# Eight groups of keys transposed by DMA, a later first output projection, and x normalised in place

## The chip, the cores and the metric

The kernel runs on one core of a Trainium2 chip. The metric is the device time of one execution in microseconds. Engines are named as the profile names them: PE is TensorE (PEld its weight loads), DVE VectorE, ACT ScalarE, POOL GpSimd, SP SyncE. SP, POOL and ACT each issue DMA transfers in their own order: a transfer that must wait holds up everything behind it on the same engine.

## The reference

```python
def reference(A_x, A_k_cache, A_v_cache, A_wq, A_wo, B_x, B_w1, B_w2, B_w3, B_w4):
    x  = A_x                                # [1, 2048, 576] bf16
    xn = _layernorm(x)
    s  = attention(xn, ...) @ wo            # 32 heads of 128, 16 key/value heads, last W = 512 keys, no mask
    # B: a mixer and an MLP on the same xn
    h  = gelu(_layernorm(xn) @ w1)          # 576 -> 576
    # the four column quarters of h are shifted along the sequence by +1, -1, +2, -2 rows
    hs = shifted(h) @ w2
    x1 = xn + hs
    h2 = gelu(_layernorm(x1) @ w3) @ w4     # 576 -> 4608 -> 576
    g  = silu(x1 + h2)
    return x + s * g
```

Each key/value head ("group" below) serves two query heads.

## The kernel before

**Blocks and slots.** The 2048 rows are four query blocks of 512. Attention runs through 4 x 32 = 128 slots, one for each block and head. A slot holds four score matmuls (`stage_s`, L541, 128x512 each), the query projection of the next head (`stage_q`, L507 and L522), sixteen products of probabilities and values (`stage_v`, L560), and, on ACT, four exponentials. The output o of a head is transposed by a DMA on SP into a tile of `oT_pool` (`stage_t`, L573).

**What fills the slots.** The program is written out by hand: `at(u, fn)` puts a step into slot u and `pe(u, atoms)` puts matmuls there, which are dealt out between the slot's own. The steps are the loads of weights, keys, values and x, layernorms, transposes, and the output projection of the block before (`wo_groups`, matmuls at L269): five lists of 32 or 128 matmuls, `main` for each of four row tiles and `rem` for the last 64 columns. For block 0 they stand in slots 34 to 38, for blocks 1 and 2 from the second slot of the block after on. wo itself comes in eight loads on POOL (`load_wo`), each behind `late`: a tiny POOL copy that reads a probability tile of the slot, so that the transfer isn't issued before that slot is reached. The slots for these are 2, 8, 16, 20, 23, 27, 29 and 31. What is queued behind such a copy on POOL waits as well.

**Keys.** Groups 0 to 3 are transposed at the launch. Groups 4 to 15 lie in a stage buffer and are transposed by PE, four transposes a group (`prep_k`, L372) and one DVE copy from PSUM (L376), in slot 2g - 3. Group g is first used in slot 2g.

**Buffers.** `stage_pool` has three buffers of 512 x 640 values. They hold, in turn, the loaded keys, the loaded x of a block, the output projection's result (`so_t`) and, for blocks 2 and 3, the transposed normalised rows for the mixer (`xnnT`, `tr2` at L261); blocks 0 and 1 have `xnnT_pool`. x is loaded into the stage buffer and normalised into `xn_b`. The tail columns 512 to 576 are stored twice in `xn_b` and `xm_b`, after the whole row.

**Mixer.** After slot 127: `b1_pair` and `b1_rest` (first layer; the last 16 columns of each quarter go through `hq` by a DMA transpose on SP, L827), `shifts` (L834, four DVE copies from hq into `hs`, and a DMA on SP that doubles hs, L835), `b2_pair` and `b2_rest` (second layer). Their order is a list with `aside` steps between. w2 (`w2_m`) is loaded by POOL behind a gate copy that waits for the last oT. At the end of the mixer come the last three lists of the output projection of block 3 (L269), and then a gate on POOL (L926) that waits for the last `hs`.

**MLP.** The pools of attention and mixer are closed, and in their memory lie nine sets of weights (`w3_s`, `w3r_s`, `w4_s`, which the profile writes w_s and w3r_s), loaded in order on POOL (L948 w3, L952 the last 64 rows of w3 in two loads, L955 w4). PE runs `up` (L996) and `down` (L1033). SP reloads s and x for the end (L965, L967).

Of the kernel before, what the change touches and what calls it, by code (L numbers as in the profile page):

```python
# [8 lines left out]
P = 128  # L9
# [22 lines left out]
def kernel(  # L32
# [14 lines left out]
    nc = tc.nc  # L47
# [68 lines left out]
    def layernorm_steps(pool, dsts, srcs, twice=False):  # L116
        n = len(srcs)
        hw = D // 2
        st_ = {}

        def stats(i):
            if i == 0:
                st_["mv"] = pool.tile([P, n, 2], FP32, name="ln_mv")
            st = pool.tile([P, 2, 6], FP32, name="ln_st")
            for j in range(2):
                tc.keep_in_program_order(
                    nc.vector.bn_stats(out=st[:, j, :], in_=srcs[i][:, j * hw:(j + 1) * hw]))
            nc.vector.bn_aggr(out=st_["mv"][:, i, :], in_=st[:])

        def inv():  # L130
            st_["r"] = rsqrt_newton(pool, st_["mv"][:, :, 1], n)

        def apply(i):
            parts = [(dsts[i], srcs[i])]
            if twice:
                parts = [(dsts[i][:, 0:D], srcs[i]), (dsts[i][:, D:DP], srcs[i][:, NF * P:D])]
            for dst, src in parts:
                nc.vector.tensor_scalar(out=dst, in0=src, scalar1=st_["mv"][:, i, 0:1],
                                        scalar2=st_["r"][:, i:i + 1], op0=ALU.subtract, op1=ALU.mult)

        return ([lambda i=i: stats(i) for i in range(n)] + [inv] + [lambda i=i: apply(i) for i in range(n)])
# [82 lines left out]

    octx = ctx.enter_context(ExitStack())
    wo_sb = octx.enter_context(tc.tile_pool(name="a_wo", bufs=1, side="right")).tile([P, Hq, D], BF16, name="wo_sb")
    oT_pool = octx.enter_context(tc.tile_pool(name="oT_pool", bufs=36, side="right"))
    fence_pool = ctx.enter_context(tc.tile_pool(name="fence", bufs=2))
    tctx = ctx.enter_context(ExitStack())
    xnnT_pool = tctx.enter_context(tc.tile_pool(name="xnnT_pool", bufs=2))  # L230
    stage_pool = tctx.enter_context(tc.tile_pool(name="stage_pool", bufs=3))
    so_t, oT_t, xnnT = {}, {}, {}
    w1_all = xT_b[0][:].rearrange("p k q -> p (k q)")
    w1_m = w1_all[:, 0:NF * D].rearrange("p (k m) -> p k m", k=NF)
    w1_p = w1_all[:, NF * D:NF * D + 2 * P].rearrange("p (j m) -> p j m", j=2)
    w1_tail = B_w1[NF * P:D, :]
    gate = keep.tile([1, 1], BF16, name="gate")

# [12 lines left out]
    def stage():  # L251
        return stage_pool.tile([P, DP * TB], BF16, name="stage")

    def stage_rows():
        return stage()[:, 0:TB * D].rearrange("p (t d) -> p t d", t=TB)

    def tr2(b, tt):
        if tt == 0:
            xnnT[b] = (xnnT_pool.tile([P, DP * TB], BF16, name="xnnT") if b < 2 else stage())[:].rearrange(
                "p (k t) -> p k t", k=NDC)  # L260
        nc.sync.dma_start(out=xnnT[b][:, :, tt * P:(tt + 1) * P], in_=xm_b[b % 2][:, tt, :], transpose=True)  # L261

    FLAG_OPS = (ALU.max, ALU.min)
# [1 line left out]
    def wo_groups(qb, bank, eng):  # L265
        st = {}

        def mm(ps, h, tt, lo, hi):
            nc.tensor.matmul(ps, lhsT=oT_t[qb * Hq + h][:, tt, :], rhs=wo_sb[:, h, lo:hi], start=(h == 0),  # L269
                             stop=(h == Hq - 1))  # L270

        def main(tt, h):
            if tt == 0 and h == 0:
                so_t[qb] = stage_rows()
            if h == 0:
                st[tt] = bank([P, M0], "pswo")
            mm(st[tt][:, :], h, tt, 0, M0)
            if h == Hq - 1:
                nc.scalar.activation(out=so_t[qb][:, tt, 0:M0], in_=st[tt][:, :], func=ACT.Copy, scale=0.5)
                if qb == NB - 1 and tt == TB - 1:  # L280
                    store()

        def store():
            eng.dma_start(out=rows(s_dram, qb * TB, TB), in_=so_t.pop(qb)[:, :, :])

        def rem(tt, h):
            if tt == 0 and h == 0:
                st["pr"] = bank([P, TB, R0], "pswr")
            mm(st["pr"][:, tt, :], h, tt, M0, D)
            if tt == TB - 1 and h == Hq - 1:  # L290
                nc.scalar.activation(out=so_t[qb][:, :, M0:D], in_=st["pr"][:, :, :], func=ACT.Copy, scale=0.5)
                if qb < NB - 1:
                    store()

        return [[lambda tt=tt, h=h: main(tt, h) for h in range(Hq)] for tt in range(TB)] + [
            [lambda tt=tt, h=h: rem(tt, h) for tt in range(TB) for h in range(Hq)]]


    with ExitStack() as actx:
# [5 lines left out]
        kT = res.tile([P, Hkv, W], BF16, name="kT")  # L305
        v_sb = res.tile([P, Hkv, KCH, VW], BF16, name="v_sb")
        NWQ = 2
        PLAIN = 4
        wq_b = [res.tile([P, NDC, 4 * Dh], BF16, name=f"wq_b{i}") for i in range(NWQ)]
        ri_b = res.tile([P, Hq, TB], FP32, name="ri_b")  # L310
# [13 lines left out]
        x_t = {}  # L324

        def load_x(b, eng):
            xb = stage_rows()
            x_t[b] = []
            for tt in range(TB):
                xt = xb[:, tt, :]  # L330
                t = b * TB + tt
                eng.dma_start(out=xt, in_=x2[t * P:(t + 1) * P, :])
                x_t[b].append(xt)
# [31 lines left out]
        def prep_k(g):  # L365
# [11 lines left out]

            return [lambda kc=kc: tr(kc) for kc in range(KCH)]

        x_t[0] = []  # L380
        x_first = stage_rows()
        hw = D // 2
        nc.scalar.dma_start(out=x_first[:, 0, hw:D], in_=x2[0:P, hw:D])
        nc.sync.dma_start(out=x_first[:, 0, 0:hw], in_=x2[0:P, 0:hw])
# [240 lines left out]

        for b in range(1, NB):
            for i, group in enumerate(wo_atoms(b - 1)):
                pe(b * Hq + (2 if b == 1 else 1) + i, group)
        for b in range(NB):
            cell = []  # L630

            def ln2_step(i, b=b, cell=cell):
                if not cell:
                    cell.append(ln2_stats_steps(b))
                cell[0][i]()

            for i in range(TB + 1):
                at(ln2_at[b] + i // 2, lambda i=i, f=ln2_step: f(i))
            if b + 1 < NB:
                at(x_at[b], lambda b=b: late(pT_t[x_at[b]][0][0:1, 0:1], lambda: load_x(b + 1, nc.gpsimd)))  # L640
                u1 = ln1_at[b]
                later(u1, lambda b=b: ln1_steps(b + 1), 3, apart=4 if b == 1 else 0)
                for tt in range(TB):
                    at(u1 + (3 + tt, 5, 3 + tt // 2)[b], lambda b=b, tt=tt: tr1(b + 1, tt))
            for tt in range(TB):
                at(tr2_at[b] - 2 + tt // 2, lambda b=b, tt=tt: ln2_apply(b, tt))
                at(tr2_at[b] + tt, lambda b=b, tt=tt: tr2(b, tt))
        wo_last = wo_atoms(NB - 1)[0:2]
        wo_last = wo_last[0][0:Hq - 1] + wo_last[1][0:8] + [wo_last[0][Hq - 1], flag_rows] + wo_last[1][8:]
        pe(U - 1, wo_last[0:10])  # L650
# [1 line left out]
        pe(U + 1, wo_last[22:])  # L652
        at(1, rest_twice)
        at(3 * Hq + 12, load_w1)
        pe_late = []
        at(4, lambda: load_k(2))
        at(12, lambda: load_k(3))
        for g in range(Hkv):
            if g % 2 == 0 and g >= 4:
                at(max(2 * g - 8, 3), lambda g=g: load_v(g // 2))  # L660
            if g > 3:
                pe_late.append((2 * g - 3, g))
        for j in range(2, NB * 8):
            at(4 * (j - 1) - 1, lambda j=j: load_wq(j))
        for i, u in enumerate((2, 8, 16, 20, 23, 27, 29, 31)):
            at(u, lambda i=i, u=u: late(pT_t[u][0][0:1, 0:1], lambda: load_wo(i)))
        for b in range(NB):
            at((b + 1) * Hq + 1, lambda b=b: row_range(b))
# [59 lines left out]
    with ExitStack() as bctx:  # L728
# [18 lines left out]
        mctx = ExitStack()  # L747
        mres = pool("m_res", 1, at=mctx)
        w1_q = mres.tile([P, 4, rsz], BF16, name="w1_q")
        w2_m = mres.tile([P, 4, D], BF16, name="w2_m")  # L750
        w2_q = mres.tile([P, D], BF16, name="w2_q")
        hb = mres.tile([P, 4, HW], BF16, name="hb")
        hq = mres.tile([P, HW], BF16, name="hq")
# [112 lines left out]
            nc.vector.tensor_tensor(out=x1, in0=pr[1], in1=gs[:], op=ALU.add)  # L866

        with tc.manual_schedule(engines={SP, POOL, PE, DVE, ACTE}):
            e = small.tile([P, 1], FP32, name="nr_e")
            nc.scalar.activation(out=e[:], in_=so_t[NB - 1][:, 1, 0:1], func=ACT.Gelu_apprx_tanh)  # L870
            for half in range(2):
                nc.gpsimd.dma_start(out=w1_q[HALVES[half], :, :],
                                    in_=w1_tail.rearrange("p (g s) -> p g s", g=4)[:, :, P:c4])
            nc.gpsimd.tensor_copy(out=gate[:, :], in_=oT_t[NB * Hq - 1][0:1, 0, 0:1])
            by_g = B_w2.rearrange("(g s) d -> g s d", s=c4)
            nc.gpsimd.dma_start(out=w2_m[:], in_=by_g[:, 0:P, :].rearrange("g s d -> s g d"))
            for half in range(2):
                for g in range(4):
                    p0 = half * DR + g * rsz
                    nc.gpsimd.dma_start(out=w2_q[p0:p0 + rsz, :], in_=by_g[g, P:c4, :])  # L880
            for t in (hb[:, :, OFF - PAD:OFF], hb[:, :, OFF + S:OFF + S + PAD], hq[:, OFF - PAD:OFF],
                      hq[:, OFF + S:OFF + S + PAD], *[t[:, :, R0:] for t in h4]):
                nc.gpsimd.memset(t, 0.0)
# [3 lines left out]
                   (b2_pair, 3)]  # L887
            ops = [(f, b, p) for f, b in ops for p in range(2)]
            aside = {0: [lambda: b1_rest(0)], 1: [lambda: b1_rest(1)], 2: [lambda: b1_rest(2)],
                     3: [lambda: b1_rest(3), lambda: shifts(0)], 6: [lambda: shifts(1)], 8: [lambda: shifts(2)],  # L890
                     10: [lambda: shifts(3)]}
            pend = None
            for k in range(len(ops) + 1):
# [467 lines left out]
```

## Time and profile before

| | |
|---|---|
| runs shown, us | 827.32, 820.60, 831.24; median 827.32 |
| profiled execution, us | 820.89 |
| its span, us | 819.4 |
| mean granted clock of TensorE | 0.999 |
| PE busy | 806.8 us, 98% |
| DVE, ACT, POOL busy | 449.8, 444.7, 125.5 us |
| bytes by DMA | 79.94 MB, mean 98 GB/s |

The span is the time from the first to the last instruction of the profiled execution; the rest of its time lies outside it. Busy times of engines overlap and are not added up: what counts is which engine is waited for in each stage. In rows of instructions the columns are: start and duration in us, engine, line and operation, output and inputs, count, and in brackets the idle time before and what ended it. A row "DMA to landing" gives the time from issue to the last byte: shortest, median and longest of the DMAs asked for.

### The profile page before, as it was taken

What the parts mean: (1) busy time and instruction counts of PE and PEld (TensorE: products, weight loads), DVE (VectorE), ACT (ScalarE), POOL (GpSimd) and SP (SyncE); (2) the same over time, 40 slices, a digit from 0 to 9 for tenths busy, and PEclk for the clock granted to TensorE, in tenths of its full rate; (3) what the DMA queues carried; (4) which work ended last, traced back from release to release, by engine and by line L of the source; (5) the groups of instructions that cost most, each with busy time, mean ns of one, the idle gap of its engine ahead of it and who ended that gap; (6) DMA issues with size and microseconds to landing.
All of it is one profiled execution on the core that took longest, in us unless ns stands there. A gap on an engine that the chain in (4) does not pass through costs nothing. (4 is left out here: it accounts for less than half of the span.)

```text
span 819.4 us, 19998 instructions
## 1 busy us (share of the span) xinstructions
PE 806.8 (98%) x8205; PEld 528.2 (64%) x8287; DVE 449.8 (55%) x1387; ACT 444.7 (54%) x798; POOL 125.5 (15%) x212
## 2 busy tenths in 40 slices
PE   8999999999999999999999999999999999999997
PEld 5666654656654666645666546555568888888855
DVE  6878644468832579621566526643246636655413
ACT  7888852688833788833888642032233323334520
POOL 3343301111101111100210031155000000000000
PEclk9999999999999999999999999999999999999999
DMA  7999952374721538810674232299100310230101
GB/s 198 164 210 209 200 105 58 91 136 104 136 55 42 113 83 151 159 49 14 132 128 85 47 67 65 61 354 213 53 2 17 87 49 16 48 88 16 44 15 38
DMA packets 131502, 79.94 MB, mean 98 GB/s; under 512 B 107824, under 2 KB 121680, under 8 KB 131408
## 3 DMA queue, kind: packets, MB, share of 16 engines
q1 hardware_dynamic: 117328, 38.54, 26.1%
q0 software_dynamic: 12832, 38.85, 18.8%
q8 instruction: 65, 1.06, 0.6%
q10 hardware_dynamic: 1248, 1.25, 0.5%
q14 instruction: 29, 0.24, 0.2%
HBM read 46.89 MB, written 6.93 MB: 66 GB/s over the span
## 5 line engine op out<-in xcount | busy, mean ns | idle before, releaser
L545 ACT ACTIVATE pT<-sc 128x512 bf16<-128x512 f32 x512 | 287.2, 598 | 98.0 <-PE sc L541 81.6
L560 PEld LDWEIGHTS <-pT 128*128 128x128 bf16 x2048 | 134.5, 98 | 52.8 <-issue 11.5
L541 PE MATMUL sc<-qT,kT 128*128 128x512 bf16 x495 | 165.1, 379 | 0.1
L560 PE MATMUL po<-v_sb,pT 128*128 128x129 bf16 x2048 | 158.2, 220 | 1.0
L996 PE MATMUL ph<-xT_b,w_s 64*128 64x512 bf16 x976 | 140.9, 376 | 0.0
L1033 PE MATMUL pm<-w_s,h 64*128 64x512 bf16 x864 | 134.9, 377 | 0.0
L522 PE MATMUL psq<-xT_b,wq_b 128*128 128x512 bf16 x463 | 123.6, 379 | 2.3
L1033 PEld LDWEIGHTS <-h 64*128 64x128 bf16 x1728 | 102.0, 94 | 27.1
L1014 ACT ACTIVATE h<-ph 128x512 bf16<-128x512 f32 x67 | 39.4, 597 | 138.2 <-PE ph L996 130.6
L565 DVE TENSOR_TENSOR o<-po,ri_b 128x256 bf16<-128x256 f32 x256 | 108.0, 422 | 6.8 <-DVE ri_b L564 0.3
L1033 PE MATMUL pr<-w_s,h 64*128 64x64 bf16 x864 | 111.3, 189 | 0.0
L269 PE MATMUL pswo<-wo_sb,oT 128*128 128x512 bf16 x434 | 101.3, 379 | 0.6
L996 PEld LDWEIGHTS <-w_s 64*128 64x128 bf16 x1152 | 85.3, 94 | 22.3 <-issue 0.6
L269 PEld LDWEIGHTS <-oT 128*128 128x128 bf16 x1024 | 64.6, 98 | 54.3
L522 PEld LDWEIGHTS <-wq_b 128*128 128x128 bf16 x506 | 49.4, 98 | 57.4 <-issue 0.8
L532 DVE CAST qT<-psq 128x512 bf16<-128x512 f32 x64 | 44.1, 689 | 76.5 <-PE psq L507 45.7
L530 DVE TENSOR_TENSOR qT<-psq,rq 128x512 bf16<-128x512 f32 x62 | 42.8, 690 | 62.3 <-ACT pT L545 53.0
L1012 DVE COPY hx<-ph 128x512 f32<-128x512 f32 x55 | 38.1, 692 | 54.7 <-PE ph L996 54.7
L339 POOL DMA_DIRECT2D wq_b<-in_A_wq_dram x30 | 23.2, 772 | 280.0 <-PE sc L541 280.0
L564 DVE RECIPROCAL ri_b<-po 128x2 f32<-128x2 f32 x256 | 42.3, 165 | 34.5 <-PE po L560 29.2
L541 PEld LDWEIGHTS <-kT 128*128 128x128 bf16 x512 | 46.3, 98 | 20.8 <-DVE qT L532 0.3
L512 ACT ACTIVATE rq<-sc 128x512 f32<-128x512 f32 x62 | 33.6, 594 | 8.0 <-PE sc L507 8.0
(171 smaller groups left out, 729.7 us busy)
## 6 DMA issues: line engine op xcount, KB each, us to landing
wq_b<-in_A_wq_dram POOLq DMA_DIRECT2D x30, 512.0 KB, 4.8
wo_sb<-in_A_wo_dram POOLq DMA_DIRECT2D x8, 576.0 KB, 5.6
w_s<-in_B_w_dram POOLq DMA_DIRECT2D x9, 512.0 KB, 9.6
w_s<-in_B_w_dram POOLq DMA_DIRECT2D x10, 288.0 KB, 7.0
w_s<-in_B_w_dram POOLq DMA_DIRECT2D x4, 576.0 KB, 9.4
s_b<-s_dram SPq DMA_DIRECT2D x4, 576.0 KB, 5.5
x_b<-in_A_x_dram SPq DMA_DIRECT2D x4, 576.0 KB, 9.0
out_dram<-o SPq DMA_DIRECT2D x15, 144.0 KB, 1.8
```

Source lines behind the costliest of these rows:

```text
L269: nc.tensor.matmul(ps, lhsT=oT_t[qb * Hq + h][:, tt, :], rhs=wo_sb[:, h, lo:hi], start=(h == 0), stop=(h == Hq - 1))
L522: nc.tensor.matmul(psq[:, :], lhsT=w[:, kc, hh * Dh:(hh + 1) * Dh], rhs=xT_b[qb % 2][:, kc, :], start=(kc == 0 and not (two and hh == 1)), ...
L530: behind["qT"] = nc.vector.tensor_tensor(out=qT[:, :], in0=psq[:, :], in1=rq_t.pop(u)[:, :], op=ALU.add)
L532: nc.vector.tensor_copy(out=qT[:, :], in_=psq[:, :])
L541: nc.tensor.matmul(sc[:, :], lhsT=kT[:, g, kc * P:(kc + 1) * P], rhs=qT_t[u][:, :], start=True, stop=True)
L545: behind["exp"] = nc.scalar.activation(out=pT[:, :], in_=sc[:, :], func=ACT.Exp, scale=SCALE)
L560: nc.tensor.matmul(po[:, j, :], lhsT=pTs[kc][:, tt * P:(tt + 1) * P], rhs=v_sb[:, g, kc, 0:Dh + 1], start=(kc == 0), stop=(kc == KCH - 1))
L564: nc.vector.reciprocal(out=ri, in_=po[:, :, Dh])
L565: nc.vector.tensor_tensor(out=o[:, t0:t0 + 2, :], in0=po[:, :, 0:Dh], in1=ri.unsqueeze(2).to_broadcast([P, 2, Dh]), op=ALU.mult)
L996: nc.tensor.matmul(ps[i][:, :], lhsT=lhsT, rhs=xT[half, kc, :], start=first, stop=last, skip_group_check=True)
L1014: nc.scalar.activation(out=h3[:, :], in_=src[:, :], func=ACT.Gelu_apprx_tanh)
L1033: nc.tensor.matmul(out, lhsT=h3_t[b, fc][half, tt * P:(tt + 1) * P], rhs=w4_s[fc // WS][half, fc % WS, lo:hi], start=key not in started, s ...
```

## The change

Four edits:

1. Keys of groups 8 to 15 are transposed by DMA on SP (`tr_k`) instead of PE and DVE, groups 8 to 11 in slots 8 to 11, and groups 12 to 15 in slots 16 to 19. Groups 4 to 7 remain on PE.
2. The output projection of block 0 moves from slots 34 to 38 to slots 43 to 47, its eight weight loads from slots 2 to 31 to slots 14 to 39, and `oT_pool` grows from 36 to 46 buffers.
3. x is loaded into `xn_b` and normalised there; so the tail columns are written ahead of the whole row. `stage_pool` has two buffers, the output projection's result a pool of its own with one (`so_pool`), and `xnnT` of blocks 0 and 1 comes from `stage_pool`. The transposes into `xnnT` of blocks 2 and 3 move from slots 86 to 95 to the start of the mixer, into tiles of its own. `w2_m` lies in `xT_b[1]` and is loaded in slot 127; the gate before it is gone.
4. The shifted copies of block 0 (`shifts(0)`) stand ahead of `b1_rest(3)`.

```diff
             if twice:
-                parts = [(dsts[i][:, 0:D], srcs[i]), (dsts[i][:, D:DP], srcs[i][:, NF * P:D])]
+                parts = [(dsts[i][:, D:DP], srcs[i][:, NF * P:D]), (dsts[i][:, 0:D], srcs[i])]
...
-    oT_pool = octx.enter_context(tc.tile_pool(name="oT_pool", bufs=36, side="right"))
+    oT_pool = octx.enter_context(tc.tile_pool(name="oT_pool", bufs=46, side="right"))
...
-    xnnT_pool = tctx.enter_context(tc.tile_pool(name="xnnT_pool", bufs=2))
-    stage_pool = tctx.enter_context(tc.tile_pool(name="stage_pool", bufs=3))
+    stage_pool = tctx.enter_context(tc.tile_pool(name="stage_pool", bufs=2))
+    so_pool = tctx.enter_context(tc.tile_pool(name="so_pool", bufs=1))
...
+    w2_m = xT_b[1][:].rearrange("p k q -> p (k q)")[:, 0:4 * D].rearrange("p (k m) -> p k m", k=4)
...
-    def tr2(b, tt):
+    def tr2(b, tt, home=None):
         if tt == 0:
-            xnnT[b] = (xnnT_pool.tile([P, DP * TB], BF16, name="xnnT") if b < 2 else stage())[:].rearrange(
-                "p (k t) -> p k t", k=NDC)
+            xnnT[b] = (home or stage())[:].rearrange("p (k t) -> p k t", k=NDC)
...
-                so_t[qb] = stage_rows()
+                so_t[qb] = so_pool.tile([P, TB, D], BF16, name="so")
...
+        KDMA = 8
...
-            xb = stage_rows()
...
-                xt = xb[:, tt, :]
+                xt = xn_b[b][:, tt, 0:D]
...
+        def tr_k(g):
+            nc.sync.dma_start(out=kT[:, g, :].rearrange("d (kc p) -> d kc p", kc=KCH),
+                              in_=kst_t[g // 4][:, (g % 4) * W:(g % 4 + 1) * W], transpose=True)
+
...
-        x_first = stage_rows()
+        x_first = xn_b[0][:, :, 0:D]
...
-                pe(b * Hq + (2 if b == 1 else 1) + i, group)
+                pe(b * Hq + (11 if b == 1 else 1) + i, group)
...
-                at(tr2_at[b] + tt, lambda b=b, tt=tt: tr2(b, tt))
+                if b < 2:
+                    at(tr2_at[b] + tt, lambda b=b, tt=tt: tr2(b, tt))
...
+        at(U - 1, lambda: nc.gpsimd.dma_start(out=w2_m, in_=w2_by_g[:, 0:P, :].rearrange("g s d -> s g d")))
...
-            if g > 3:
+            if 3 < g < KDMA:
                 pe_late.append((2 * g - 3, g))
+            if g >= KDMA:
+                at(g if g < 12 else g + 4, lambda g=g: tr_k(g))
...
-        for i, u in enumerate((2, 8, 16, 20, 23, 27, 29, 31)):
+        for i, u in enumerate((14, 22, 27, 30, 33, 35, 37, 39)):
             at(u, lambda i=i, u=u: late(pT_t[u][0][0:1, 0:1], lambda: load_wo(i)))
...
-        w2_m = mres.tile([P, 4, D], BF16, name="w2_m")
...
+            for b in range(2, NB):
+                home = mres.tile([P, DP * TB], BF16, name=f"xnnT{b}")
+                for tt in range(TB):
+                    tr2(b, tt, home)
...
-            nc.gpsimd.tensor_copy(out=gate[:, :], in_=oT_t[NB * Hq - 1][0:1, 0, 0:1])
-            by_g = B_w2.rearrange("(g s) d -> g s d", s=c4)
-            nc.gpsimd.dma_start(out=w2_m[:], in_=by_g[:, 0:P, :].rearrange("g s d -> s g d"))
...
-                     3: [lambda: b1_rest(3), lambda: shifts(0)], 6: [lambda: shifts(1)], 8: [lambda: shifts(2)],
+                     3: [lambda: shifts(0), lambda: b1_rest(3)], 6: [lambda: shifts(1)], 8: [lambda: shifts(2)],
```

More of the change, by code (lines that the diff above doesn't have):

```diff
@@ L235 @@
     w1_p = w1_all[:, NF * D:NF * D + 2 * P].rearrange("p (j m) -> p j m", j=2)
+    w2_m = xT_b[1][:].rearrange("p k q -> p (k q)")[:, 0:4 * D].rearrange("p (k m) -> p k m", k=4)
+    w2_by_g = B_w2.rearrange("(g s) d -> g s d", s=c4)
     w1_tail = B_w1[NF * P:D, :]
@@ L252, in stage @@
         return stage_pool.tile([P, DP * TB], BF16, name="stage")
-    def stage_rows():
-        return stage()[:, 0:TB * D].rearrange("p (t d) -> p t d", t=TB)
-    def tr2(b, tt):
+    def tr2(b, tt, home=None):
         if tt == 0:
-            xnnT[b] = (xnnT_pool.tile([P, DP * TB], BF16, name="xnnT") if b < 2 else stage())[:].rearrange(
-                "p (k t) -> p k t", k=NDC)
+            xnnT[b] = (home or stage())[:].rearrange("p (k t) -> p k t", k=NDC)
         nc.sync.dma_start(out=xnnT[b][:, :, tt * P:(tt + 1) * P], in_=xm_b[b % 2][:, tt, :], transpose=True)
@@ L879 @@
                     p0 = half * DR + g * rsz
-                    nc.gpsimd.dma_start(out=w2_q[p0:p0 + rsz, :], in_=by_g[g, P:c4, :])
+                    nc.gpsimd.dma_start(out=w2_q[p0:p0 + rsz, :], in_=w2_by_g[g, P:c4, :])
             for t in (hb[:, :, OFF - PAD:OFF], hb[:, :, OFF + S:OFF + S + PAD], hq[:, OFF - PAD:OFF],
```

## The prediction

> **What bounds the kernel now.** I read the page of the profile first: busy times, then the slices with the granted clock.
>
> ```profile
> span 819.4 us, 19998 instructions
> PE 806.8 (98%) x8205; PEld 528.2 (64%) x8287; DVE 449.8 (55%) x1387; ACT 444.7 (54%) x798; POOL 125.5 (15%) x212
> PEclk9999999999999999999999999999999999999999
> ```
>
> TensorE (PE) is busy for 806.8 of 819.4 us at an undisturbed clock, so only two things can move the end: PE instructions that come or go, and waits in front of PE. The second view is the table of stretches: launch, four attention slots of block 0 with key transposes (67.87 to 79.49), four of block 1 without (155.85 to 167.02), the end of the mixer, and the start of the MLP. After the length come the busy times of PE, PEld, DVE, ACT and POOL, then clock, DMA share and GB/s.
>
> ```profile
> 3.30:12.00 8.70, 7.70 (x89) 5.87 (x88) 7.24 (x21) 5.83 (x13) 0.14 (x1) 1.00 1.03 278
> 67.87:79.49 11.62, 11.52 (x108) 7.23 (x109) 11.41 (x48) 9.97 (x19) 3.83 (x7) 1.00 0.95 163
> 155.85:167.02 11.17, 11.06 (x101) 6.78 (x101) 7.32 (x21) 9.88 (x20) 1.98 (x3) 1.00 0.60 139
> 20.00:70.00 50.00, 49.53 (x458) 31.17 (x467) 39.94 (x130) 43.03 (x78) 22.32 (x37) 1.00 1.17 196
> 526.00:532.00 6.00, 5.95 (x28) 2.71 (x28) 0.00 (x0) 0.33 (x1) 2.73 (x4) 1.00 0.68 136
> 532.00:540.00 8.00, 8.00 (x75) 3.51 (x75) 1.69 (x5) 2.80 (x5) 4.67 (x7) 1.00 1.04 350
> ```
>
> PE fills every stretch except the launch. The other engines have room everywhere but for DVE in block 0 (11.41 of 11.62 us). The DMA engines are full (share 1.0 or more) at the launch, in block 0, and at the start of the MLP, so those are the places where a moved transfer can hurt.
>
> **The change part by part.** *Keys of groups 8 to 15.* Eight groups lose four transposes each: 32 matmuls, 32 weight loads and 8 DVE copies. The matmul's own duration is not the price, because it overlaps its neighbours:
>
> ```profile
> L372 PE MATMUL ps_k<-ident,stage 128*128 128x128 bf16 x48 | 8.6, 219 | 0.0
> 60.68 0.22 PE L372 MATMUL ps_k<-ident,stage 128*128 128x128 bf16 x1
> 60.74 0.38 PE L541 MATMUL sc<-qT,kT 128*128 128x512 bf16 x1
> 61.68 0.27 PE L372 MATMUL ps_k<-ident,stage 128*128 128x128 bf16 x2
> 61.79 0.38 PE L541 MATMUL sc<-qT,kT 128*128 128x512 bf16 x1
> ```
>
> One transpose pushes the next score matmul back by 0.06 us and two by 0.11, so 32 are worth 32 x 0.055 = 1.76 us. The two stretches of four slots say the same: 11.62 - 11.17 = 0.45 us for 8 transposes, and 4 x 0.45 = 1.8. I take **-1.8 us**. What would undo it is DVE, the fullest engine there. Each removed copy also frees it:
>
> ```profile
> L376 DVE COPY kT<-ps_k x11: 404/414/416, 27.1 to 85.4; 128x512 bf16<-128x512 bf16 x11
> L573 SPq DMA_TRANSPOSE oT<-o x128: 1188/1191/2262, 15.8 to 468.8; - x128
> DMA to landing us min/median/max: 2.4/3.4/12.7
> ```
>
> DVE falls to 11.41 - 2 x 0.41 = 10.6 us per four slots, below PE's 11.17. In place of the transposes SP issues eight DMA transposes of the size of the existing oT ones: 8 x 1.2 = 9.5 us of SP's queue, over eight slots of 11.17 / 4 = 2.8 us. Their data is wanted eight or more slots after the issue, 22 us, against a landing of at most 12.7 us. On SP only oT transposes and x transposes stand behind them, and the first oT is now read at slot 43. Cost 0.
>
> *Output projection of block 0 and its weights.* The same matmuls run in slots 43 to 47 instead of 34 to 38, the weights in eight later loads, the oT pool grows from 36 to 46. PE work is only moved: 0. The oT of heads 46 and 47 of the sequence reuse buffers whose last reader runs in slot 47; SP may stand for a slot or two there, and what is queued behind it (oT) has many slots of cover. Two side effects remain, and they are not free.
>
> The first is at the launch. The first weight load stood behind a gate on POOL, and the v loads of groups 4 and 5 stood behind it:
>
> ```profile
> 2.90 0.53 POOL L404 MEMSET v_sb<- 128x512 bf16 x1
> 16.48 0.18 POOL L240 COPY gate<-pT 1x1 bf16<-1x1 bf16 x1 [13.04 <-ACT pT L545]
> 17.47 1.49 POOL L362 DMA_DIRECT2D v_sb<-in_A_v_cache_dram  x2
> L397 SPq DMA_DIRECT2D wq_b<-in_A_wq_dram x1: 472/472/472, 3.4 to 3.4; - x1
> DMA to landing us min/median/max: 4.9/5.0/5.2
> 9.18 2.32 PE L695 MATMUL psq<-xT_b,wq_b 128*128 128x512 bf16 x9
> ```
>
> Without that gate the two v loads (256 KB) go out at about 3.4 us, into a stretch whose DMA share is 1.03 at 278 GB/s. 256 KB at that rate are 0.94 us. The first half of wq lands at 3.9 + 4.9 = 8.8 us and is read at 9.18, so 0.4 of the 0.94 is covered: the bounds are 0 (all of it lands behind wq) and +0.55. I take **+0.3**.
>
> The second is at the start of the MLP. The weights w3 and w4 come in nine sets; set 0 is loaded at 506 us, and set 1 as soon as its memory is free. With 36 buffers set 1's first load waits for the thirteenth of the last 32 output-projection matmuls; with 46 the oT pool lies over set 1 and it waits for the last.
>
> ```profile
> 529.02 0.76 POOL L948 DMA_DIRECT2D w_s<-in_B_w_dram  x1 [20.09 <-PE pr L269]
> 529.76 1.21 POOL L952 DMA_DIRECT2D w3r_s<-in_B_w_dram  x2
> 532.75 1.04 PE L996 MATMUL ph<-xT_b,w_s 64*128 64x512 bf16 x8
> 536.72 1.04 PE L996 MATMUL ph<-xT_b,w_s 64*128 64x512 bf16 x8
> 537.58 0.75 PE L996 MATMUL ph<-xT_b,w3r_s 64*128 64x512 bf16 x2
> 537.95 0.60 PE L1033 MATMUL pm<-w_s,h 64*128 64x512 bf16 x2
> DMA to landing us min/median/max: 4.5/4.5/4.5
> DMA to landing us min/median/max: 6.4/7.0/7.5
> DMA to landing us min/median/max: 3.5/3.7/3.8
>   PEld L996: 0.5, 1
> ```
>
> The landing rows are of set 1's w3 (issued 529.02), of the two loads of its last rows (529.76 and 530.37), and of the same two loads of set 0, when nothing else is in flight. The wait ends 19 matmuls later; 28 of them take 6.00 us in the table, 0.214 each: 19 x 0.214 = 4.1 us. Already now PE meets set 1 with nothing to spare: its second half waits until 530.37 + 7.5 = 537.9 (the 0.5 us wait of PEld), and PE goes on at 537.95. After the change the first load goes at 533.1, the last rows at 533.9 and 534.5. The lower bound is w3's 4.5 us: 537.6 against 536.72, a stall of 0.9 us (the last rows then land at 534.5 + 3.8 = 538.3, in time for their use 0.9 us later). The upper bound for landings as of set 1 now is 534.5 + 7.5 = 542.0 against 537.95, +4.05. The reloads of s and x by SP (four of 576 KB) are already in flight when it is issued and the table shows 350 GB/s at share 1.04 for 532 to 540, so the contended row is the nearer: **+3.0**. Later sets are issued in the order of POOL's queue and arrive at the distance of one set; I add nothing for them.
>
> *x normalised in place, stage pool of 2, so pool of 1.* No instruction more or less; the tail columns are written ahead of the rest. The x loads wait for no buffer. 0.
>
> *Transposes of the normalised rows of blocks 2 and 3, w2, shifts.* Eight transposes on SP move from block 3 to the mixer's start, ahead of hq; w2 is loaded one slot before attention ends instead of behind a gate; block 0's shifted copies go ahead of block 3's small products on DVE.
>
> ```profile
> 468.76 1.20 SPq L573 DMA_TRANSPOSE oT<-o  x1
> 481.58 7.89 SPq L827 DMA_TRANSPOSE hq<-h  x4
> L261 SPq DMA_TRANSPOSE xnnT<-xm_b x8: 1267/1272/1901, 109.5 to 172.4; - x8
> 488.57 1.28 DVE L834 COPY hs<-hq 32x512 bf16<-32x512 bf16 x4 [0.80 <-DMA hq<-h]
> 491.01 0.38 PE L765 MATMUL pm<-w_q,hs 64*128 64x512 bf16 x1
> 491.87 0.39 PE L765 MATMUL pm<-w_q,hs 64*128 64x512 bf16 x1 [0.48 <-DMA hs<-hs]
> ```
>
> SP is free at 469.96; eight transposes of 1.27 us end at 480.1, 1.5 us before hq is wanted; the four of block 2, which are read first, have left by 475.1. PE waits for hs: its two matmuls start 0.86 us apart where 0.214 is the rate, a loss of 0.65. The shifted copies end 1.3 us after hq lands, and now skip the two small DVE operations in front. But they waited 0.80 us for hq itself, so the gain is there only if hq lands sooner; bounds -0.65 and 0. I take **-0.65**, since POOL's small transfers, which were in flight beside that hq, now go earlier.
>
> **Sum:** +0.3 - 1.8 + 3.0 - 0.65 = +0.85 us. The profiled execution took 820.89 us (span 819.4 and 1.5 around it): **821.7 us** for one like it. The runs shown are 820.6 to 831.24, with that execution near the bottom, 6.4 below their median. The mean of the four (the three runs and the profiled one) is 825.0, so I expect a median of 825.0 + 0.85 = **825.9**.
>
> **The rivals.** *A: the gains stand.* Set 1 takes its share of the DMA engines at once and lands as set 0 did: stall 0.9 instead of 3.0, sum -1.25, 819.6 for the profiled kind. For it: w3 of set 1 took 4.5 us both beside the reloads and alone. Against it: w3's last rows took twice as long beside them. The Trainium skill, page "DMA: Bandwidth & Descriptors", section "Queues, rings and completion order", says that each DMA engine goes round between the queues packet by packet, so POOL's loads would not stand behind SP's whole backlog; no row here separates that from a backlog.
>
> *B: set 1 waits its turn, slower.* Place: the same load. Set 2's w3, issued at 532.1 into the full stretch, took 10.2 us:
>
> ```profile
> DMA to landing us min/median/max: 10.2/10.2/10.2
> ```
>
> If set 1 does as badly from 533.1, it lands at 543.3 against 536.72: +6.6 instead of 3.0, sum +4.45, 825.3. It decides from a stall above 2.15 us (0.3 - 1.8 - 0.65 gives that much back). Against it: set 2 also stood behind set 1's own loads.
>
> *C: the transposes' gain is swallowed.* DVE at 10.6 of 11.17 us keeps PE at the old pace in block 0: sum +2.65, 823.5. The table of stretches speaks against it.
>
> *D: the DMA transposes of the keys come late.* In the 20 to 70 us stretch the DMA share is 1.17. If each landed 25 us after its issue instead of at most 12.7, PE would wait 25 - 22 = 3 us for each of eight groups, 24 us, 845. It decides from 22 us.
>
> **How the numbers follow.** Forecast 0.45, A 0.25, B 0.15, C 0.11, D 0.04. Forecast, A, B and C lie within 2% (16.5 us, about what a measurement of this kernel can tell from no change), D is slower: faster 0.01, same 0.95, slower 0.04. For the range, the unknown costs reach from -1.55 (launch 0, stall 0.9, gains whole) over the forecast's +0.85 to B's +4.45, and single runs from 820.6 to 831.2. The low end is 820.6 - 1.55 = **819**; the high end is 831.2 plus the middle between forecast and B, 2.65: **834**. D alone is left out.
>
> **What would show it.** Right: no L372 after 45 us and four-slot stretches of 11.2 us in the second half of block 0; two v loads of POOL at 3.4 us and the first wq product a few tenths late; no PE wait for hs; POOL's second w3 load at the last output-projection matmul and a PE wait of about 3 us on it. Wrong: that wait under 1 us or over 5, waits on kT or qT in block 0, or hq issued after its values are ready.

## The result, and the profile after

The changed kernel is slower by about 1%: 830.29 us (median of 22 runs, 825.63 to 835.53) against 820.60 us for the kernel before in as many. The ratio is 1.0103, with a 95% interval of 1.0078 to 1.0128. Of the 22 runs of the kernel before 15 lie between 819.8 and 822.6 us and two at 827 and 831; the five between 841 and 867 are left out of the ratio, as runs far above the rest are below, and no profile here shows their cause. The changed kernel spreads evenly over 10 us, which is itself a finding: see the wait for wq below.

The profiled execution took 832.92 us, 12.0 more in span than the one before. The page of the profile after, and its list of what PE waited for (in total, times, longest):

```profile
span 831.4 us, 20017 instructions
PE 813.7 (98%) x8255; PEld 449.3 (54%) x8255; DVE 444.2 (53%) x1379; ACT 445.7 (54%) x798; POOL 125.3 (15%) x211
PEclk9999999999999999999999999989999999999999
...
PE ph L1002 <- DMA w_s<-in_B_w_dram: 5.0, 1, 5.0
PE psq L524 <- DMA wq_b<-in_A_wq_dram: 3.4, 1, 3.4
PE pm L770 <- ACT hb L796: 2.4, 1, 2.4
```

Three waits, 10.8 us together, stand where the kernel before had none (wq) or short ones: the prediction showed those at the mixer and the MLP, 0.5 us each. The PE timeline gives the marks between them. Of each pair the first row is the kernel before, the second the kernel after: the first scores of slot 0, those of slot 33, the mixer's first product, and the MLP's first product after.

```profile
11.42 1.02 PE L541 MATMUL sc<-qT,kT 128*128 128x512 bf16 x4
11.27 1.02 PE L543 MATMUL sc<-qT,kT 128*128 128x512 bf16 x4
104.77 0.59 PE L541 MATMUL sc<-qT,kT 128*128 128x512 bf16 x2
102.77 0.59 PE L543 MATMUL sc<-qT,kT 128*128 128x512 bf16 x2
478.24 1.25 PE L765 MATMUL ph<-xnnT,xT_b 64*128 64x512 bf16 x10
481.88 1.25 PE L770 MATMUL ph<-stage,xT_b 64*128 64x512 bf16 x10
538.00 1.04 PE L1002 MATMUL ph<-xT_b,w_s 64*128 64x512 bf16 x8
```

After minus before, these rows differ by -0.15 us at slot 0, -2.0 at slot 33, +3.6 at the mixer, +5.25 at the MLP (538.00 against 532.75) and +12.0 at the end. So the gain in block 0 is there, and 5.6 us are lost in blocks 1 to 3, 1.6 in the mixer, and 6.75 from the MLP's start on. Each of the three losses has one place:

```profile
134.63 1.21 PE L524 MATMUL psq<-xT_b,wq_b 128*128 128x512 bf16 x4 [3.42 <-DMA wq_b<-in_A_wq_dram]
495.32 1.91 PE L770 MATMUL pm<-xT_b,hb 64*128 64x512 bf16 x16 [2.36 <-ACT hb L796]
547.09 1.89 PE L1002 MATMUL ph<-xT_b,w_s 64*128 64x512 bf16 x8 [5.03 <-DMA w_s<-in_B_w_dram]
```

The waits do not add up to the losses, and the table of stretches says why. The columns are as before: length, busy times of PE, PEld, DVE, ACT and POOL, granted clock, DMA share, GB/s.

```profile
66.50:77.74 11.24, 11.24 (x104) 6.74 (x102) 11.06 (x48) 9.88 (x20) 2.91 (x5) 1.00 0.76 139
135.00:140.00 5.00, 5.00 (x25) 2.12 (x23) 1.28 (x3) 1.09 (x2) 0.00 (x0) 0.66 1.42 89
496.00:500.00 4.00, 4.00 (x72) 2.40 (x70) 2.64 (x8) 0.24 (x1) 0.00 (x0) 1.00 0.05 11
547.00:550.00 3.00, 2.91 (x16) 1.07 (x18) 0.48 (x2) 0.00 (x0) 2.26 (x4) 0.50 1.07 379
```

After the waits of 3.42 and 5.03 us PE runs at a granted clock of 0.66 and 0.50 for some microseconds; after the one of 2.36 us at 1.00. The first line shows four slots of block 0 without transposes, 11.24 us where they took 11.62.

**The wait for wq.** POOL's timeline before slot 43. The weights that PE waits for are those issued at 118.34, and they landed 15.2 to 16.2 us later. The last row is the landing of the wq loads that the kernel before issued from 105 to 125 us:

```profile
113.46 2.15 POOL L330 DMA_DIRECT2D xn_b<-in_A_x_dram  x4 [0.31 <-issue]
116.06 0.76 POOL L410 DMA_DIRECT2D wo_sb<-in_A_wo_dram  x1 [0.28 <-issue]
118.34 0.76 POOL L337 DMA_DIRECT2D wq_b<-in_A_wq_dram  x1 [1.52 <-PE sc L543]
DMA to landing us min/median/max: 15.2/15.7/16.2
DMA to landing us min/median/max: 4.7/5.6/5.7
```

The kernel before had long slots here (its output projection ran in 34 to 38, 9.5 us a slot) and loaded x at 129 us. Now slots 34 to 42 are short, and hold loads of wo and x and the transposes that used to have three times as long.

**The mixer.** DVE and ACT, whose order is fixed:

```profile
491.58 1.28 DVE L839 COPY hs<-hq 32x512 bf16<-32x512 bf16 x4 [1.49 <-DMA hq<-h]
492.89 0.42 DVE L829 COPY gs<-pr 128x256 f32<-128x256 f32 x1
493.88 0.42 ACT L831 ACTIVATE h<-gs 128x256 bf16<-128x256 f32 x1 [3.51 <-DVE gs L830]
494.20 1.07 ACT L796 ACTIVATE hb<-pm 128x512 bf16<-128x512 f32 x2
```

The shifted copies stand first now and wait 1.49 us for hq. The two small DVE operations wait behind them, ACT's gelu of those waits 3.51 us, and behind that gelu stands the hb that PE needs. The hq for which the copies wait landed sooner than in the kernel before, not later. Its time from issue to landing, before and after:

```profile
DMA to landing us min/median/max: 5.2/5.2/5.2
DMA to landing us min/median/max: 4.5/4.5/4.5
```

The copies ended 11.0 us after the mixer's first product (492.86 - 481.88), against 11.6 before (489.85 - 478.24).

**The MLP's start.** POOL issues set 1 after the last output-projection matmul, while SP's reloads of s and x, issued from 534.9 on, are in flight:

```profile
538.37 0.75 POOL L954 DMA_DIRECT2D w_s<-in_B_w_dram  x1 [23.61 <-PE pr L267]
DMA to landing us min/median/max: 8.7/8.7/8.7
```

538.37 + 8.7 = 547.07, the moment at which PE goes on.

### The profile page after: what moved, and what is told of

It reads as the page before. It is cut to its first block, busy times and chain, and to the rows that moved or that the text cites. A ratio compares the mean times of both kernels' runs of the same rounds, so it can differ in the third digit from the quotient of the medians.

```text
span 831.4 us, 20017 instructions
## 1 busy us (share of the span) xinstructions
PE 813.7 (98%) x8255; PEld 449.3 (54%) x8255; DVE 444.2 (53%) x1379; ACT 445.7 (54%) x798; POOL 125.3 (15%) x211
## 5 line engine op out<-in xcount | busy, mean ns | idle before, releaser
L543 PE MATMUL sc<-qT,kT 128*128 128x512 bf16 x512 | 170.9, 379 | 0.1
L524 PE MATMUL psq<-xT_b,wq_b 128*128 128x512 bf16 x506 | 129.9, 379 | 3.4 <-DMA wq_b<-in_A_wq_dram 3.4
L1002 PE MATMUL ph<-xT_b,w_s 64*128 64x512 bf16 x976 | 126.3, 379 | 5.0 <-DMA w_s<-in_B_w_dram 5.0
L1039 PE MATMUL pm<-w_s,h 64*128 64x512 bf16 x864 | 121.1, 379 | 0.0
L267 PE MATMUL pswo<-wo_sb,oT 128*128 128x512 bf16 x448 | 103.8, 381 | 0.0
L1039 PEld LDWEIGHTS <-h 64*128 64x128 bf16 x1728 | 61.0, 95 | 66.1 <-issue 1.4
L1039 PE MATMUL pr<-w_s,h 64*128 64x64 bf16 x864 | 82.3, 190 | 0.0
L1002 PEld LDWEIGHTS <-w_s 64*128 64x128 bf16 x1152 | 47.7, 95 | 62.7 <-DMA w_s<-in_B_w_dram 5.5
```

Of the source, the lines that this page charges most:

```text
L524: nc.tensor.matmul(psq[:, :], lhsT=w[:, kc, hh * Dh:(hh + 1) * Dh], rhs=xT_b[qb % 2][:, kc, :], start=(kc == 0 and not (two and hh == 1)), ...
L543: nc.tensor.matmul(sc[:, :], lhsT=kT[:, g, kc * P:(kc + 1) * P], rhs=qT_t[u][:, :], start=True, stop=True)
L1002: nc.tensor.matmul(ps[i][:, :], lhsT=lhsT, rhs=xT[half, kc, :], start=first, stop=last, skip_group_check=True)
L1039: nc.tensor.matmul(out, lhsT=h3_t[b, fc][half, tt * P:(tt + 1) * P], rhs=w4_s[fc // WS][half, fc % WS, lo:hi], start=key not in started, s ...
```

## The experiments

All times are medians of 4 to 12 runs, and ratios are against the kernel before on the same chip. Most runs undo a part of the change; one puts a part of it alone into the kernel before.

**Output projection of block 0 back, with its loads.**

```diff
-    oT_pool = octx.enter_context(tc.tile_pool(name="oT_pool", bufs=46, side="right"))
+    oT_pool = octx.enter_context(tc.tile_pool(name="oT_pool", bufs=36, side="right"))
-                pe(b * Hq + (11 if b == 1 else 1) + i, group)
+                pe(b * Hq + (2 if b == 1 else 1) + i, group)
-        for i, u in enumerate((14, 22, 27, 30, 33, 35, 37, 39)):
+        for i, u in enumerate((2, 8, 16, 20, 23, 27, 29, 31)):
```

> The changed kernel with the output projection of block 0 in slots 34 to 38, its weight loads in slots 2 to 31 and 36 oT buffers, as before. Theory (three separate waits of PE, two of them from the later projection): the wait for wq (3.4 us) in slot 43 and the one for w3 (5.0 us) at the MLP's start both go, and with them the low clock behind each; the mixer's wait (2.4 us, 1.6 net) stays, and the 2.0 us gained up to slot 33 stay. Span 819.4 - 2.0 + 1.6 = 819.0, so within 0.2% of the kernel before. Rival (the DMA transposes of the keys, or x in place with two stage buffers, crowd the DMA engines): the wait for wq stays at 3 us or more, span about 824.

Measured: 852.54 us, ratio 1.0363 (1.0304 to 1.0422). Neither theory: instead of giving back 8 us, undoing this edit costs over 20 more. The wait for w3 is gone, as the theory said (36 buffers), but up to the start of block 1 PE now waits 13.0 us in its profile for wq (7.3) and for block 1's transposed x (5.7).

**Only the loads of wo back.**

```diff
-        for i, u in enumerate((14, 22, 27, 30, 33, 35, 37, 39)):
+        for i, u in enumerate((2, 8, 16, 20, 23, 27, 29, 31)):
```

> The changed kernel with only the eight loads of wo back in slots 2 to 31; the projection's matmuls stay in slots 43 to 47, with 46 oT buffers. Theory (the four loads of slots 33 to 39 stand ahead of wq on POOL's queue and fill the DMA engines): the wait for wq falls under 0.5 us, the slot that holds it takes 10.2 instead of 15.4 us, span 831.4 - 5.2 = 826.2; the w3 wait stays at 5.0. Rival (the matmuls' place: slots 34 to 42 are short now, so oT and xnnT transposes and the x load of block 2 come in a third of the time): a wait for wq of 2 us or more stays, span above 828.5.

Measured: 851.89 us, ratio 1.0326 (1.0285 to 1.0367). The wait in slot 43 is gone as the theory said (PE's timeline has none from 110 to 160 us; the output projection begins in slot 43, at 157 us). The wq loads of this place, issued at 131.3 and 142.5 us here, landed in time:

```profile
DMA to landing us min/median/max: 4.8/5.8/7.2
```

In the five profiles with the late loads of wo and x in its place the slowest wq load there took longer: 16.2 us in the changed kernel; 10.8, 12.4, 12.3 and 13.7 in the runs below with the old order of copies, with 48 buffers, with both, and with the keys on PE. PE comes to it some 13 us after the issue, so only 13.7 and 16.2 show as waits. But block 0 breaks down. Its timeline and the stretch from 30 to 100 us, here, in the kernel before and in the changed one:

```profile
56.33 1.89 PE L524 MATMUL psq<-xT_b,wq_b 128*128 128x512 bf16 x4 [3.55 <-DMA wq_b<-in_A_wq_dram]
71.85 1.35 PE L543 MATMUL sc<-qT,kT 128*128 128x512 bf16 x3 [2.32 <-ACT pT L547]
103.67 1.61 PE L524 MATMUL psq<-xT_b,wq_b 128*128 128x512 bf16 x4 [3.77 <-DMA wq_b<-in_A_wq_dram]
...
30.00:100.00 70.00, 61.93 (x511) 35.73 (x509) 47.23 (x165) 49.37 (x91) 22.40 (x38) 0.93 1.17 142
30.00:100.00 70.00, 69.37 (x635) 43.28 (x646) 56.93 (x193) 60.15 (x110) 26.59 (x45) 1.00 1.12 193
30.00:100.00 70.00, 70.00 (x635) 42.39 (x633) 55.09 (x188) 61.38 (x113) 24.65 (x41) 1.00 0.87 185
```

In these 70 us the kernel before had the DMA engines full (1.12) without the key transposes. With them and the early loads the share is 1.17, but the rate falls from 193 to 142 GB/s. The changed kernel has 0.87. So the late loads of wo are what makes room for the key transposes: the two edits are one.

**The keys alone, in the kernel before.**

```diff
+            if g >= KDMA:
+                at(g if g < 12 else g + 4, lambda g=g: tr_k(g))
```

(with `KDMA = 8`, `tr_k`, and PE's transposes kept for groups 4 to 7.)

> The kernel before with only the eight key transposes by DMA. Theory (they find no room on the DMA engines while wo is loaded in the same slots): wq lands 12 us or more after its issue between 30 and 100 us, PE waits for it several times, 20 to 30 us more than before: 840 to 850. Rival (the crowd of the two runs with early loads of wo comes from x in place or from two stage buffers): only the transposes' gain shows, 819, with wq landing as before in 5 to 11 us.

Measured: 842.98 us, ratio 1.0245 (1.0207 to 1.0283), 20 us more. The time fits the theory, and the rival falls: the breakdown needs neither x in place nor the smaller stage pool. The wait is not the forecast one. In the profiled execution, at 852 us the slowest of the four, PE waited longest for

```profile
PE psq L527 <- DMA xT_b<-xn_b: 18.7, 1, 18.7
PE psq L527 <- DMA wq_b<-in_A_wq_dram: 4.2, 2, 3.4
```

The first is block 1's normalised x, which SP transposes. Behind the keys and the oT on SP these transposes left from 92.9 us on instead of 78.1, and landed 11.7 to 18.4 us after their issue instead of 2.7 to 6.4. The wq loads landed after 8.7 us (median), 18.8 at most. So that the keys crowd the DMA engines is shown; which transfer PE then waits for differs from run to run.

**The keys on PE again, in the changed kernel.**

```diff
-        KDMA = 8
+        KDMA = 16
```

> The changed kernel with all keys of groups 4 to 15 transposed on PE again (the late loads of wo and all else as changed). Theory: PE's 32 transposes cost 1.8 us again up to slot 28, the wait for wq near 130 us stays since it comes long after the last key: 829 + 1.8 = 831. Rival (the key transposes on SP push the oT transposes behind them back, and these crowd the slots from 33 on): the wait for wq goes, 827 or less.

Measured: 829.30 us (828.21 to 829.85, four runs), ratio 1.0103 (1.0088 to 1.0118). Between the two: the 1.7 us in block 0 are lost again, as its slots show,

```profile
11.64 1.02 PE L543 MATMUL sc<-qT,kT 128*128 128x512 bf16 x4
104.86 0.59 PE L543 MATMUL sc<-qT,kT 128*128 128x512 bf16 x2
PE psq L524 <- DMA wq_b<-in_A_wq_dram: 0.9, 1, 0.9
```

(93.2 us from slot 0 to slot 33, where the changed kernel takes 91.5), but the wait for wq is 0.9 us in this profile, and the total does not move. A wq load still takes 13.7 us to land, so it is late without the key transposes too; whether they add to the 16.2 us, or this was only a mild execution, is left open.

**The order of the shifted copies back.**

```diff
-                     3: [lambda: shifts(0), lambda: b1_rest(3)], ...
+                     3: [lambda: b1_rest(3), lambda: shifts(0)], ...
```

> The changed kernel with block 0's shifted copies behind block 3's small products again, as before. Theory (the copies wait for hq on DVE, the small products' two DVE operations stand behind them, the gelu of those on ACT, and the next hb behind that gelu): PE's wait for hb (2.36 us) goes, the wait for hs comes back with about 0.65 us, 1.7 us less: span 829.7. Rival (the eight transposes on SP make hq late whatever the order): the 2.4 us stay, as a wait for hs or hb, span 831.4.

Measured: 827.56 us, ratio 1.0093 (1.0068 to 1.0118). The time alone cannot part the theories, with the wait for wq scattering; the profile does:

```profile
491.04 0.39 PE L770 MATMUL pm<-w_q,hs 64*128 64x512 bf16 x1 [0.49 <-DMA hs<-hs]
```

The wait for hb is gone and hs makes PE wait as long as before. From the mixer's first product to the MLP's first it takes 55.05 us, against 54.51 in the kernel before and 56.12 in the changed one. So the order costs 1.1 us of the 1.6 here, and about half a us remains: the copies wait 1.33 us for hq, against 0.80 before, and PE another 0.30 for DVE. That the eight transposes on SP ahead of hq cost this is likely, but not shown.

**48 oT buffers, so that set 1 waits for nothing.**

```diff
-    oT_pool = octx.enter_context(tc.tile_pool(name="oT_pool", bufs=46, side="right"))
+    oT_pool = octx.enter_context(tc.tile_pool(name="oT_pool", bufs=48, side="right"))
-        o_pool = pool("o_pool", 8)
+        o_pool = pool("o_pool", 7)
```

The buffers turn round, so their number decides which memory the heads of block 3 lie on; 48 leaves that of the first two kinds of loads of set 1 free.

> The changed kernel with 48 oT buffers and 7 o buffers, which puts block 3's oT off the memory of the first two loads of set 1, so that they wait for no output-projection matmul. Theory: the w3 wait of 5.0 us and the low clock behind it go, 6.7 us less: span 824.7. Rival (the weights come late because the reloads of s and x fill the DMA engines, whenever they are asked for): the wait moves to set 1's w4 or to set 2 and costs 3 us or more, span above 828.

Measured: 822.49 us (820.79 to 826.57), ratio 1.0028 (1.0015 to 1.0041). In POOL's timeline the loads of set 1 that PE waited for (w3 and its last rows) go right behind set 0, and from 536 to 540 us, soon after the MLP's start at 535.30, the clock is full:

```profile
512.58 0.75 POOL L954 DMA_DIRECT2D w_s<-in_B_w_dram  x1
536.00:540.00 4.00, 4.00 (x40) 1.84 (x38) 1.11 (x3) 1.30 (x3) 4.00 (x7) 1.00 1.07 368
```

No later set takes the wait over. The rival falls. The mixer's wait for hb is still there, and costs more than in the changed kernel: 2.62 us, with a low clock behind it, so that the mixer takes 58.07 us.

**Both mended.** The two edits above together.

> The changed kernel with the old order of the shifted copies and with 48 oT and 7 o buffers (the two edits of the runs on the mixer and on the MLP's start together). Theory: the two waits are separate, so their gains add, 1.7 + 6.7 = 8.4 us less than the changed kernel; with its median of 829 that is 820.6, the kernel before to within 0.2%. No wait of PE for hb or w3 is left, a wait for wq near 130 us of 0 to 4 us may be. Rival: with both mended a later load or transpose becomes the next wait, and no more than 6.7 us are won: 822 or more.

Measured: 819.63 us (818.41 to 826.90), ratio 1.0007 (0.9988 to 1.0027). They add: 10.7 us together, 2.7 and 7.8 apart.

**Both mended, and x of block 2 in slot 45.**

```diff
-        x_at = (14, Hq + 4, 2 * Hq + 4)
+        x_at = (14, Hq + 13, 2 * Hq + 4)
```

> The same, with the x load of block 2 nine slots later (slot 45 instead of 36), among the long slots of the output projection. Theory (the short slots 34 to 42 hold too many transfers, and x stands on POOL's queue just ahead of two loads of wo and the wq that is late): wq lands within 10 us of its issue at 118 us, not 11 to 16, no wait for it near 130 us, and the time falls by up to 2 us against the run without this edit: 818.5 to 820. Rival (the transposes on SP alone make it late): landing 11 us or more, time unchanged.

Measured: 819.01 us (818.16 to 824.26), ratio 0.9986 (0.9974 to 0.9999). This is the only version with a ratio below 1, by 0.1%, and its interval ends just under 1. The landing of the two wq loads issued from 105 to 125 us, first without and then with this edit:

```profile
DMA to landing us min/median/max: 5.3/9.1/12.3
DMA to landing us min/median/max: 5.0/6.6/9.6
```

Of 12 runs without it four lie above 821 us, of 11 with it one does. In the two runs below that also have x in slot 45 the slowest wq load took 6.8 and 12.8 us, against 10.8 to 16.2 in the five profiles with x in slot 36. So it is likely, but not shown beyond the scatter, that the x load is part of the crowd. The median hardly moves, since most executions of the mended kernel, to judge by their times, have no wait for wq at all.

**Only the wait for set 1 left, and the same wait filled.** The old order of the copies and the late x, with 46 buffers; then with 20 idle matmuls on PE ahead of the third `up`.

```diff
+            spare = ps_h2.tile([P, QB], FP32, name="pr0")
+            for _ in range(20):
+                nc.tensor.matmul(spare[:, :], lhsT=ident[:, :], rhs=xT_b[0][:, 0, :], start=True, stop=True)
```

> The changed kernel with the old order of the shifted copies and x of block 2 loaded in slot 45, but with 46 oT buffers, so that of the long waits only the one for set 1 of w3 is left. Theory: against the run with 48 buffers (819.0) it costs the wait of 5.0 us and the low clock behind it, 6.7 us: 825.7. Rival (with the other waits gone the weights are asked for earlier relative to the reloads of s and x): the wait shrinks to 3 us, 822.

> The same with 20 matmuls that nothing reads (128x512, 4.3 us) on PE where it waits for set 1 of w3, so that PE does not stand idle. The data arrive no sooner. Theory (1.7 us of the 6.7 are the low clock that follows the idle stretch): the clock stays at 1.00 and the time falls to 824.0, 1.7 us under the run without them. Rival (the 1.7 us are later loads of sets that come late too): the time does not fall, 825.7.

Measured: 826.58 us (825.61 to 827.36) and 824.36 us (823.59 to 828.97); ratios 1.0060 (1.0038 to 1.0083) and 1.0042 (1.0018 to 1.0066). The stretch after the data arrived, without and with the idle matmuls:

```profile
541.00:544.00 3.00, 3.00 (x20) 1.14 (x18) 0.58 (x2) 0.00 (x0) 2.11 (x4) 0.50 1.07 384
541.00:544.00 3.00, 3.00 (x40) 1.44 (x38) 0.65 (x3) 0.04 (x1) 1.99 (x4) 1.00 1.07 386
```

Twice the matmuls in the same 3 us. Work that nothing needs saves 2.2 us by the medians (1.5 by the ratios), and 11 of its 12 runs lie below the fastest of the 12 without it. So of the 7.6 us that this wait costs by the medians (826.58 - 819.01, on two chips; 6.1 by the ratios) about 2 are the clock.

## Why the prediction was right or wrong, point by point

The sum put +0.85 us for an execution like the profiled one; the two profiled executions lie 12.0 apart. Up to slot 33 the kernel gained 2.0 where the sum had 1.5. Blocks 1 to 3 lost 5.6 where it had 0, the mixer lost 1.6 where it had a gain of 0.65, and from the MLP's start on 6.75 were lost where it had 3.0. The 0 is the largest miss in this execution, but the wait for wq is not in every one; over the medians the MLP's start weighs most, since mending it is worth 7.8 us (830.29 - 822.49).

- **Keys, -1.8 us: the size was right, the "cost 0" of the transposes on SP was not.** Slot 0 to slot 33 takes 93.35 us before, 91.5 after and 93.2 with the keys on PE. DVE did not hold PE up, though it was busy for 11.06 us of the four slots and not the 10.6 reckoned, so rival C falls. But the check of the transposes' landing used rows of a program without them. Alone they cost 20 us. They cost nothing only since the loads of wo moved out of the same slots, which the forecast didn't name as a condition. Nor did the danger show where rival D put it: PE never waited for keys (they landed within 6.3 us in the changed kernel), but, with early loads of wo, for wq and for the x transposes that the forecast saw standing behind the keys on SP and put at nothing.
- **Later output projection, "PE work is only moved: 0": the step that failed first.** I counted what is queued behind the moved transposes on SP, and left out what the moved loads stand ahead of on POOL. Four loads of 576 KB came into slots 33 to 39, which had become short by the very same edit. Three of them and the x load were issued from 104.9 to 116.1 us, ahead of the wq of 118.3, which landed after 16 us instead of 5.7. With the loads back it lands within 7.2; how much each transfer adds was not separated. In the profiled execution slot 43 lost 5.2 us: 3.42 of waiting and 1.7 of low clock (5 us at 0.66). The wait differs from run to run: of the profiles with the late loads and x in its place, this one has 3.4 us, that with the keys on PE 0.9, and those with the old order of copies, with 48 buffers and with both none.
- **Launch, +0.3 us: too small to tell.** The two v loads went out at 3.37 us, as foreseen, but the first wq product started at 9.03 us, not later than the 9.18 before. Slot 0 began 0.15 us earlier in this profile, and at 11.64 instead of 11.42 us in that with the keys on PE.
- **Start of the MLP, +3.0 us with bounds 0.9 and 4.05: the mechanism was right, the size was not.** The load waited for the last output-projection matmul (4.1 us later, as worked out), and rival B described the rest: w3 stood among the reloads, 8.7 us to its landing. The upper bound took w3 itself at 4.5 us as before, and added the late part only to the last rows; that 4.5 was from an issue ahead of the reloads. The loss also had a second term that no step had, the clock: 5.0 us of wait cost 6.75. This miss is the steadiest: every profile with 46 buffers has the wait (4.2 to 5.4 us) unless idle matmuls fill it, and none with 36 or 48.
- **Mixer, -0.65 us: wrong in sign.** The gain was tied to hq landing sooner, and that came true: 4.5 us after its issue, against 5.2, and the copies ended 0.6 us sooner. But they still wait 1.49 us for hq, and standing first they put two DVE operations, a gelu and hb behind that wait, and PE lost 2.36 us in place of 0.65. The prediction looked only at the copies, and as the other bound it put 0: it did not follow what is queued behind.
- **x in place, pools, transposes moved to the mixer: 0, right to within half a us.** With both waits mended the profiled span is 817.3 us, 2.1 below the kernel before, about the gain in block 0 (1.9 in that profile), so no large loss is hidden elsewhere.
- **The level.** The three runs shown and the profile were taken as a sample around 825. In 22 runs the kernel before has its median at 820.6, and the profiled execution was a typical one: the forecast for an execution like it was 821.7, and the changed kernel has 830.3. That this lies inside the range of 819 to 834 is luck: the upper end came from a single run of the kernel before at 831.2, while the forecast and rivals A to C put such an execution at 819.6 to 825.3.

Rival A fell: set 1 did not land as fast as set 0. The rule of the Trainium skill that stood beside it ("DMA: Bandwidth & Descriptors", "Queues, rings and completion order": the DMA engines go round between the queues) is not refuted by that. No run here shows how much of the 8.7 us was sharing and how much backlog.

## What to carry to other kernels

Cost a moved transfer together with everything that is queued behind it and with the length of the slots that it moves into; a stage that another edit shortens loses the slack that hid its transfers. Do not move an instruction that waits ahead of one that does not, unless its data are shown to be there by then (here they came 0.7 us sooner, and that was not enough): follow each queue behind it to the bottleneck. When a pool grows, look at whose memory it now lies on, since the number of its buffers decides which load of the next stage waits for the last reader.

## What the runs showed of the hardware

- **A wait of PE can have a tail.** After waits of 2.15 us (keys on PE) and 2.36 us (the changed kernel) the granted clock was 1.00. After 3.42 us it was 0.66 for 5 us, as much as half the clock for 3.4 us, and after 5.03 and 5.38 us 0.50 for 3 us, then 0.70 and 0.76 for another 3. In between the length of the wait did not decide: one of 2.67 us for hb (early loads of wo) left the clock at 1.00, one of 2.62 us (48 buffers) did not, as the stretches behind it show:

```profile
491.00:494.00 3.00, 3.00 (x18) 1.39 (x19) 0.21 (x1) 0.85 (x2) 0.00 (x0) 0.61 0.22 44
494.00:497.00 3.00, 3.00 (x42) 1.69 (x40) 2.35 (x7) 0.00 (x0) 0.00 (x0) 0.82 0.00 0
```

The tail cost 1.7 to 2.2 us, and idle matmuls took it away. The Trainium skill, page "TensorE: Matmul & The Clock Gate", section "Part 1: The HAM clock gate (the "warmup" mystery)", has half the clock after about 3.4 us of idleness; the trace agrees for the waits of 3.42 us and more, and differs for the one of 2.62 us.
- **Full DMA engines don't only queue, they slow down.** From 30 to 100 us the kernel before moved 193 GB/s at a share of 1.12. With eight key transposes more (early loads of wo) the share was 1.17, but the rate 142 GB/s. The loads' queue had the same share in both, 59.6% and 59.7%, and moved 9.37 MB before and 6.50 MB then; the transposes' queue moved 4.04 MB at 51.4% and 3.33 MB at 55.8%. Why both kinds of transfer slow down no run here shows. Added to the kernel before, eight transposes of 128 KB cost 20 us.
